# Attention as 64x64 matmul tiles in groups of four, with a two-bank sum for attn·v, two-step lag, and the first two expert blocks in step

## The chip, the cores and the metric

The kernel runs on one core of one Trainium2 chip. The metric is the device time of one execution in microseconds (us). Engines: TensorE (PE; its weight loads are shown apart as PEld), VectorE (DVE), ScalarE (ACT), GpSimd (POOL) and SyncE (SP, which here issues all DMAs). Each of PE, ACT, DVE and POOL works through its own list of instructions in the order in which the kernel writes them, and waits on semaphores for the others.

## The reference

Attention with a sigmoid in place of a softmax, over 8 batches, 12 heads, 448 positions and a head size of 64, and behind it a two-layer feed-forward with a gated ReLU6. All arrays are float32; the two weight matrices come to the kernel as float64 and are converted there.

```python
scores = scale * np.matmul(q, k.transpose(0, 1, 3, 2)) - np.log(S)   # S = 448
attn = 1.0 / (1.0 + np.exp(-scores))
x = np.matmul(attn, v)                       # -> 3584 tokens x 768
h = x @ w_in                                 # 768 -> 2048
g = h * np.clip(h + 3.0, 0.0, 6.0) / 6.0
out = g @ w_out                              # 2048 -> 768
```

## The kernel before, in words

**Stages.** The 3584 tokens are cut into 7 blocks of 512 for the feed-forward, while a batch has 448 tokens. So the program runs: attention of batches 0, 1 and 2; the first layer (`moe_in`, L236 ff.) of blocks 0 and 1; then, for each of batches 3 to 6, its attention and `moe_in` of one block (2 to 5); attention of batch 7; `moe_in` of block 6; and last the second layer (`moe_out`, L378 ff.) of all blocks. Results of the first layer (`g`) go to DRAM and come back for the second.

**Attention.** Two heads share the 128 partitions as a pair `p`: the one's 64 head dimensions in the upper half, the other's in the lower (`halves`). Two pairs make 7 steps `n`: a pair has 448 = 3 x 128 + 64 keys, so three whole chunks each, and one shared step that takes the last 64 keys of both pairs. A batch has 21 steps, and the whole kernel 168.

- `scores(n)` (L153) writes k·q for 128 keys of two heads into a PSUM tile `sc` of two banks. For a whole chunk these are two matmuls with 64 rows (the head size) and 128 columns (the keys), at L163, one per head; they use the upper and the lower half of the array's rows side by side. The shared step uses four matmuls of 64 rows and 64 columns, L161. Then ACT writes the sigmoid of all 2 x 448 columns as `a` to SBUF (L165).
- `av(n)` (L183) multiplies by v and sums over the keys into PSUM `pv` (one bank per pair, `pv0`/`pv1` by parity). For a whole chunk: two matmuls with 128 rows (keys) and 64 columns, L196. In the shared step: four of 64x64, L194.
- The profile shows each float32 matmul as two matmul and two weight-load records. So a whole step has 4 records in `sc` and 4 in `pv`, a shared step 8 and 8.
- When a pair's sum is complete, ACT copies it out rounded to the matmul's type (`xh`, L211), and DVE writes the rest (`xl`, L212). For batch 2 the part that belongs to block 2 waits in `pend` (L208), since block 2's buffers are still those of block 0; `flush` (L175) converts it later.

**Order.** `attention` (L271) goes in groups of `GS` = 3 steps: three `scores`, then the three `av` of the group before, so that there are three `sc` buffers (6 banks) and two `pv` banks. `moe_in` uses the same `sc` buffers for its accumulator `ph`: 18 matmuls of 128x128 by 512 for each of 16 chunks `fc`, then a ReLU on ACT (L250), DVE's product `g` (L251) and the DMA of `g`.

**First-layer weights.** The weights are converted in 32 halves (`load_wi`, L217): DMA of float64 words to `wis` (L230); then ACT (L50), five DVE operations (L51 to L57) and a POOL addition (L60), in `join_f64`; then an ACT cast (L65) and a POOL subtraction (L66) into `wi`, in `split_f32`. `ways` (L257) says when each half does its three parts; `feed` issues them between the steps. 20 halves (`NWA`) belong to the attention of batches 0 to 2, the other 12 to `moe_in(0)`, in units of `KU` = 14 matmuls.

Of the kernel before, what the change touches and what calls it, by code (L numbers as in the profile page):

```python
# [9 lines left out]
F32 = mybir.dt.float32  # L10
# [4 lines left out]
ALU = mybir.AluOpType  # L15

B, H, S, D = 8, 12, 448, 64
DM, DF = 768, 2048
P = 128
NC = S // P  # L20
NP = H // 2
NCC = DM // P
NFC = DF // P
# [5 lines left out]
NB = 3  # L29
PEND = 3 * S - 2 * T  # L30
LC = 2 * NC + 1
LB = NP // 2 * LC
GS = 3
KU = 14
NWA = 20
NWU = 1.4
GSL = 56
NWE = 12
NEA = 5
# [1 line left out]
F64_TOP = float.fromhex("0x1.dfep-96")  # L41

halves = (slice(0, D), slice(D, P))


def join_f64(nc, st, a, b):
# [41 lines left out]
def pieces(b):  # L88

    at, out = b * S, []  # L90
    while at < (b + 1) * S:
        n = min((at // T + 1) * T, (b + 1) * S) - at
        out.append((at // T, at % T, at - b * S, n))
        at += n
    return out
# [3 lines left out]
def tile_kernel(ctx: ExitStack, tc: tile.TileContext, qk, vP, wi, wo, outT):  # L99
    nc = tc.nc  # L100
# [10 lines left out]
    ph2 = ExitStack()  # L111
# [7 lines left out]
        win[g] = wins[g].enter_context(tc.tile_pool(name=f"win{g}", bufs=1, side="right"))  # L119
    xpl = ph2.enter_context(tc.tile_pool(name="xpl", bufs=1))  # L120
    att = ph2.enter_context(tc.tile_pool(name="att", bufs=1))
    ps_s = ph2.enter_context(tc.tile_pool(name="ps_s", bufs=GS, space=bass.MemoryType.PSUM))
    ps_a = ph2.enter_context(tc.tile_pool(name="ps_a", bufs=1, space=bass.MemoryType.PSUM))

    xpr.tile([P, 104], F32, name="pad")
# [7 lines left out]
    ops, at, pv, xb, pend = {}, {}, {}, {}, {}  # L133

    def load(p):
        b, hp = divmod(p, NP)
        t = att.tile([P, 2, S], F32, tag="qk", name=f"qk_{p}", bufs=4)
        v = att.tile([P, 2 * NC + 1, D], F32, tag="v", name=f"v_{p}", bufs=4)
        nc.sync.dma_start(out=t, in_=qk[b, hp])
        if p % 2 == 0:  # L140
            nc.sync.dma_start(out=v, in_=vP[b, hp])
        else:
            nc.sync.dma_start(out=v[:, : 2 * NC], in_=vP[b, hp, :, : 2 * NC])
            for j in range(2):
                nc.sync.dma_start(out=v[halves[1 - j], 2 * NC], in_=vP[b, hp, halves[j], 2 * NC])
        ops[p] = t[:, 0], t[:, 1], v

    def step(n):

        m, r = divmod(n, LC)  # L150
        return ((2 * m, 2 * m + 1), None) if r == NC else ((2 * m + (r > NC),), r % (NC + 1))

    def scores(n):  # L153
        ps, c = step(n)
        sc = ps_s.tile([P, 2, 512], F32, tag="sc", name=f"sc_{n}")
        for u, p in enumerate(ps):
            q, k, _ = ops[p]
            for j in range(2):
                if c is None:
                    out = sc[halves[j if u == 0 else 1 - j], u, :S]  # L160
                    nc.tensor.matmul(out, k[halves[j], NC * P :], q[halves[j]], start=True, stop=True)  # L161
                else:
                    nc.tensor.matmul(sc[:, j, :S], k[halves[j], c * P : (c + 1) * P], q[halves[j]], start=True, stop=True)  # L163
        a = att.tile([P, 2, S], F32, tag="a", name=f"a_{n}", bufs=2 * GS)
        nc.scalar.activation(a, sc[:, :, :S], AF.Sigmoid, bias=bias_s, scale=scale)  # L165
        at[n] = a

    def block(t, cc):
        if (t, cc) not in xb:
            pool = xpl if t % 2 else xpr  # L170
            x = pool.tile([P, 2, T], F32R, tag=f"x{t % 2}{cc}", name=f"x_{t}_{cc}")
            xb[t, cc] = x[:, 0], x[:, 1]
        return xb[t, cc]

    def flush(b, cc):  # L175

        t, c0, _, n = pieces(b)[1]
        xh, xl = (x[:, c0 : c0 + n] for x in block(t, cc))
        x = pend[b][:, cc, :n]
        nc.vector.tensor_copy(xh, x)  # L180
        nc.vector.tensor_tensor(out=xl, in0=x, in1=xh.bitcast(F32), op=ALU.subtract)

    def av(n):  # L183
        ps, c = step(n)
        a = at.pop(n)
        for u, p in enumerate(ps):
            v = ops[p][2]
            if p not in pv:
                pv[p] = ps_a.tile([P, 512], F32, tag=f"pv{p % 2}", name=f"pv_{p}")
            for j in range(2):  # L190
                out = pv[p][halves[j], :S]
                if c is None:
                    rows = halves[j if u == 0 else 1 - j]
                    nc.tensor.matmul(out, v[rows, 2 * NC], a[rows, u], start=(u == 1), stop=(u == 0))  # L194
                else:
                    nc.tensor.matmul(  # L196
                        out, v[:, j * NC + c], a[:, j],
                        start=(p % 2 == 0 and c == 0), stop=(p % 2 == 1 and c == NC - 1),
                    )
        p = ps[0]  # L200
        if c is None or (p % 2 and c == NC - 1):
            b, hp = divmod(p, NP)
            pt = pv[p]
            for u, (t, c0, q0, w) in enumerate(pieces(b)):
                if u and b == NB - 1:
                    if b not in pend:
                        pend[b] = xpl.tile([P, NCC, PEND], F32, tag="pend", name=f"pend_{b}")
                    nc.vector.tensor_copy(pend[b][:, hp, :w], pt[:, q0 : q0 + w])  # L208
                    continue
                xh, xl = (x[:, c0 : c0 + w] for x in block(t, hp))  # L210
                nc.scalar.copy(xh, pt[:, q0 : q0 + w])  # L211
                nc.vector.tensor_tensor(out=xl, in0=pt[:, q0 : q0 + w], in1=xh.bitcast(F32), op=ALU.subtract)  # L212

    wih, wil = {}, {}
    evac = []
# [17 lines left out]
        yield  # L233
        split_f32(nc, hi, lo, ab[:, :w])

    def moe_in(t):  # L236
        for fc in range(NFC):
            if t < NT - 1:
                ph = ps_s.tile([P, 2, T], F32, tag="sc", name=f"ph_{t}_{fc}")[:, 0]
            else:  # L240
                ph = ps_m.tile([P, T], F32, tag="ph", name=f"ph_{t}_{fc}")
            n = 0
            for cc in range(NCC):
                xh, xl = xb[t, cc]
                for w, x in ((wih[fc], xh), (wih[fc], xl), (wil[fc], xh)):
                    nc.tensor.matmul(ph, w[:, cc], x, start=(n == 0), stop=(n == 3 * NCC - 1))  # L246
                    n += 1
                    yield
            g = xpr.tile([P, T], F32, tag="g", name=f"g_{t}_{fc}", bufs=2)
            i1 = nc.scalar.activation(g, ph, AF.Relu, bias=bias_3, scale=1.0)  # L250
            i2 = nc.vector.scalar_tensor_tensor(out=g, in0=g, scalar=6.0, in1=ph, op0=ALU.min, op1=ALU.mult)  # L251
            evac.append((i1.ins, i2.ins))
            nc.sync.dma_start(out=gd[t][fc // GF][:, fc % GF], in_=g)


    NG0 = NB * LB // GS
    ways = []  # L257
    for n in range(2 * NFC):
        i = n * NG0 // NWA
        k = NG0 + 1 + int((n - NWA) * NWU)  # L260
        ways.append((i, i + 2, i + 3) if n < NWA else (k - 3, k, k + 1))
    way = {}

    def feed(part, i):
        for n, parts in enumerate(ways):
            if parts[part] == i:
                if part == 0:
                    way[n] = load_wi(n)
                next(way[n], None)

    def attention(first, last, w_in=False):  # L271

        for s in range(first, last, GS):
            i = (s - first) // GS
            if w_in:
                feed(0, i)
                if s == 0:
                    load(1)
                feed(1, i)
            for n in range(s, s + GS):  # L280
                scores(n)
            if w_in:
                feed(2, i)
            for n in range(s - GS, s):
                if n >= first:
                    av(n)
            for n in range(s, s + GS):
                m, r = divmod(n, LC)
                if r in (0, NC) and (p := 2 * m + 2 + (r == NC)) < B * NP:
                    load(p)  # L290
        for n in range(last - GS, last):
            av(n)

    engines = {mybir.EngineType.PE, mybir.EngineType.Activation, mybir.EngineType.DVE, mybir.EngineType.Pool}
    with tc.manual_schedule(engines=engines):
        load(0)
        attention(0, NB * LB, True)
        for n, _ in enumerate(moe_in(0)):
            i, r = divmod(n, KU)
            if r == 0:  # L300
                for part in range(3):
                    feed(part, NG0 + i)
        for n, _ in enumerate(moe_in(1)):
            if n % (3 * NCC) == 0 and n // (3 * NCC) < NCC:
                flush(NB - 1, n // (3 * NCC))
        for b in range(NB, B):
            attention(b * LB, (b + 1) * LB)
            if b < B - 1:
                for _ in moe_in(b - 1):
                    pass  # L310
# [45 lines left out]
    for n, _ in enumerate(moe_in(NT - 1)):  # L356
        if n % NWE == 0:
            next(early, None)
        g, r = divmod(n, fcm * GF)
# [72 lines left out]
```

## Time and profile before

| | us |
|---|---|
| median of 3 runs | 1212.27 (1211.23 to 1212.77) |
| the profiled execution's own time | 1211.91 |
| its span, first to last instruction | 1210.1 |
| TensorE busy in it | 1200.8 (99%) |
| attention of batches 0 to 2 | 4.27 to 112.37 |
| first layer of blocks 0 and 1 | 112.37 to 243.17 |
| attention of batch 3 | 243.17 to 278.59 |
| last attention (batch 7) starts | 646.87 |
| first layer of block 6 | 683.58 to 749.16 |
| second layer | 749.16 to 1206.41 |

How to read the rows: a group's row names the line, the engine, the operation, the tiles (written <- read), the shape and the count; behind the bar stand the busy time in us and the mean of one in ns, then the idle time of the engine ahead of these instructions and what ended it. Matmuls overlap, so the mean of one matmul is longer than the distance between two. In the chain of work that ended last, each piece has its start, its length and its line; pieces follow each other without a gap. A row of windows has start:end, length, then busy time and count for PE, PEld, DVE, ACT and POOL, the granted clock, the DMA share and GB/s.

### The profile page before, as it was taken

The numbers are of one execution on the slowest core, as the hardware profiler recorded it, in microseconds if no ns is written. First come the engines' busy times: TensorE is split into PE (matmuls) and PEld (weight loads), VectorE is DVE, ScalarE is ACT, GpSimd is POOL, SyncE is SP. The second block draws the span as 40 slices with busy tenths as digits, with TensorE's granted clock in tenths as the row PEclk, the third lists the DMA queues.
The fourth block names the chain that finished last, engine by engine and source line by source line (L and its number), as shares of the span: only waits on it lengthen the run. The fifth ranks groups of instructions, "written<-read, shape, count | busy, mean of one in ns | idle before, by whom it ended". The sixth has DMA issues, their size and how long they took to land.

```text
span 1210.1 us, 13738 instructions
## 1 busy us (share of the span) xinstructions
PE 1200.8 (99%) x5568; PEld 852.4 (70%) x5568; DVE 366.3 (30%) x606; ACT 372.1 (31%) x500; POOL 64.6 (5%) x70
## 2 busy tenths in 40 slices
PE   8999999999999999999999999999999999999998
PEld 3334888837855863883785588888888888888887
DVE  2556742111111111111111389871120303030300
ACT  6886321162144135116214445340110202020200
POOL 1333520000000000000000000000000000000000
PEclk9999999999999999999999999999999999999999
DMA  7666521132133114113212278532040404040000
GB/s 240 193 193 182 158 96 61 69 114 77 61 96 94 70 68 122 61 66 114 80 61 80 79 233 296 211 118 108 29 163 27 157 27 165 27 166 18 27 27 27
DMA packets 52000, 128.84 MB, mean 106 GB/s; under 512 B 9184, under 2 KB 15328, under 8 KB 48352
## 3 DMA queue, kind: packets, MB, share of 16 engines
q1 hardware_dynamic: 51936, 127.95, 31.5%
q8 instruction: 44, 0.72, 0.2%
q14 instruction: 20, 0.16, 0.0%
HBM read 87.56 MB, written 40.37 MB: 106 GB/s over the span
## 4 chain that ended last, share of the span: by engine, by line
PE 99%; DMA 0%; DVE 0%; ACT 0%; issue 0%
PE ph L246 38%; PE po L385 38%; PE sc L163 10%; PE pv L196 10%; PE pv L194 2%; PE sc L161 2%; DMA qk<-qk 0%; DVE o L392 0%; DVE x L212 0%; ACT x L211 0%
## 5 line engine op out<-in xcount | busy, mean ns | idle before, releaser
L246 PE MATMUL ph<-x,wi 128*128 128x512 f32 x2016 | 458.8, 389 | 1.3 <-DVE x L212 1.3
L246 PEld LDWEIGHTS ph<-x,wi 128*128 128x128 f32 x2016 | 377.9, 188 | 83.9 <-issue 3.5
L385 PE MATMUL po<-gl,woh 128*128 128x512 f32 x672 | 261.5, 389 | 0.0
L385 PE MATMUL po<-gh,wol 128*128 128x512 f32 x672 | 261.4, 389 | 0.0
L385 PE MATMUL po<-gh,woh 128*128 128x512 f32 x672 | 261.4, 389 | 0.0
L165 ACT ACTIVATE a<-sc,bias_s 128x896 f32<-128x896 f32 x168 | 157.1, 1007 | 52.4 <-PE sc L163 52.1
L250 ACT ACTIVATE g<-ph,bias 128x512 f32<-128x512 f32 x112 | 77.1, 689 | 294.9 <-PE ph L246 287.9
L251 DVE SCALAR_TENSOR_TENSOR g<-g,ph 128x512 f32<-128x512 f32 x112 | 77.0, 688 | 287.1 <-ACT g L250 287.1
L385 PEld LDWEIGHTS po<-gl,woh 128*128 128x128 f32 x672 | 126.1, 188 | 26.7 <-DVE gl L346 0.4
L345 ACT CAST gh<-gr 128x2048 fp32r<-128x2048 f32 x28 | 53.6, 1915 | 296.5 <-PE po L385 294.8
L385 PEld LDWEIGHTS po<-gh,wol 128*128 128x128 f32 x672 | 126.1, 188 | 26.2
L385 PEld LDWEIGHTS po<-gh,woh 128*128 128x128 f32 x672 | 126.1, 188 | 26.1
L163 PE MATMUL sc<-qk 64*128 64x448 f32 x576 | 127.9, 568 | 4.3 <-DMA qk<-qk 4.3
L196 PE MATMUL pv<-a,v 128*64 128x448 f32 x576 | 122.4, 550 | 0.0
L392 DVE TENSOR_SCALAR o<-po 128x512 f32<-128x512 f32 x42 | 29.0, 690 | 294.9 <-PE po L385 294.9
L163 PEld LDWEIGHTS sc<-qk 64*128 64x128 f32 x576 | 50.6, 189 | 77.7 <-issue 37.3
L196 PEld LDWEIGHTS pv<-a,v 128*64 128x64 f32 x576 | 35.6, 136 | 80.4 <-issue 77.3
L212 DVE TENSOR_TENSOR x<-pv,x 128x448 fp32r<-128x448 f32 (+6 forms) x78 | 32.7, 420 | 195.0 <-ACT x L211 195.0
L346 DVE TENSOR_TENSOR gl<-gr,gh 128x2048 fp32r<-128x2048 f32 x28 | 64.1, 2290 | 29.2 <-ACT gh L345 29.2
L211 ACT CAST x<-pv 128x448 fp32r<-128x448 f32 (+6 forms) x78 | 28.8, 369 | 37.3 <-DVE x L212 14.4
L60 POOL TENSOR_TENSOR wis<-wis 128x384 f32<-128x384 f32 x32 | 32.3, 1010 | 95.6 <-DVE wis L57 95.6
L66 POOL TENSOR_TENSOR wi<-wis,wi 128x384 fp32r<-128x384 f32 x32 | 32.5, 1024 | 7.9 <-ACT wi L65 7.7
(31 smaller groups left out, 307.3 us busy)
## 6 DMA issues: line engine op xcount, KB each, us to landing
gd<-g SPq DMA_DIRECT2D x112, 256.0 KB, 2.4
gr<-gd SPq DMA_DIRECT2D x28, 1024.0 KB, 5.3
qk<-qk SPq DMA_DIRECT2D x48, 448.0 KB, 3.4
wis<-wi SPq DMA_DIRECT2D x32, 384.0 KB, 3.3
ws<-wo SPq DMA_DIRECT2D x24, 512.0 KB, 4.8
outT<-o SPq DMA_DIRECT2D x42, 256.0 KB, 2.0
v<-vP SPq DMA_DIRECT2D x24, 224.0 KB, 2.5
v<-vP SPq DMA_DIRECT2D x24, 192.0 KB, 2.8
```

The lines of the kernel that those rows point to most:

```text
L60: nc.gpsimd.tensor_tensor(out=a, in0=a, in1=b, op=ALU.add)
L66: nc.gpsimd.tensor_tensor(out=lo, in0=a, in1=hi.bitcast(F32), op=ALU.subtract)
L163: nc.tensor.matmul(sc[:, j, :S], k[halves[j], c * P : (c + 1) * P], q[halves[j]], start=True, stop=True)
L165: nc.scalar.activation(a, sc[:, :, :S], AF.Sigmoid, bias=bias_s, scale=scale)
L196: nc.tensor.matmul(out, v[:, j * NC + c], a[:, j], start=(p % 2 == 0 and c == 0), stop=(p % 2 == 1 and c == NC - 1),)
L212: nc.vector.tensor_tensor(out=xl, in0=pt[:, q0 : q0 + w], in1=xh.bitcast(F32), op=ALU.subtract)
L246: nc.tensor.matmul(ph, w[:, cc], x, start=(n == 0), stop=(n == 3 * NCC - 1))
L250: i1 = nc.scalar.activation(g, ph, AF.Relu, bias=bias_3, scale=1.0)
L251: i2 = nc.vector.scalar_tensor_tensor(out=g, in0=g, scalar=6.0, in1=ph, op0=ALU.min, op1=ALU.mult)
L345: nc.scalar.copy(gh, gr)
L346: nc.vector.tensor_tensor(out=gl, in0=gr, in1=gh.bitcast(F32), op=ALU.subtract)
L385: nc.tensor.matmul(po[t, ec], w[:, fc], x[:, u], start=(fc == 0 and n == 0), stop=(fc == NFC - 1 and n == 2))
```

## The change

1. `scores` and `av` use 64x64 tiles only, in the order `TILES` = (rows 0, columns 0), (1, 1), (0, 1), (1, 0). In `scores` the chunk's 128 keys are two column halves, and each head (row half) has its own bank. In `av` the 128 keys are two row halves; each writes a bank of its own, so that a pair has two banks (`pv0_p`, `pv1_p`) that hold two partial sums. Four `pv` banks and two `sc` buffers (4 banks) fill the PSUM.
2. When a pair is complete, ACT copies the one partial sum to SBUF (`y`), DVE adds the other from PSUM (`x`), then DVE casts (`xh`) and subtracts (`xl`). For the pending part the addition goes to `pend`.
3. `attention` goes step by step: `scores(s)`, then `av(s - 2)` (`LAG` = 2), in place of groups of three.
4. `moe_in(0, 1)` runs both blocks together: chunk `fc` of block 0, chunk `fc` of block 1, next chunk. All six `flush` come after it; before, they stood within `moe_in(1)`.
5. The weight schedule is counted in steps: 14 halves in the attention of batches 0 to 2, 18 in `moe_in(0, 1)` at one per 21 matmuls.

```diff
-GS = 3
+LAG = 2
 KU = 14
-NWA = 20
-NWU = 1.4
+NWA = 14
+NWU = 1.5
...
+TILES = ((0, 0), (1, 1), (0, 1), (1, 0))
...
-    ps_s = ph2.enter_context(tc.tile_pool(name="ps_s", bufs=GS, space=bass.MemoryType.PSUM))
+    ps_s = ph2.enter_context(tc.tile_pool(name="ps_s", bufs=2, space=bass.MemoryType.PSUM))
...
     def scores(n):
...
-        for u, p in enumerate(ps):
+        for r, j in TILES:
+            p = ps[-1 if c is None and r != j else 0]
             q, k, _ = ops[p]
...
+            at_k = slice(NC * P, S) if c is None else slice(c * P + j * D, c * P + (j + 1) * D)
+            out = sc[halves[j], int(r != j) if c is None else r, :S]
+            nc.tensor.matmul(out, k[halves[r], at_k], q[halves[r]], start=True, stop=True)
+        a = att.tile([P, 2, S], F32, tag="a", name=f"a_{n}", bufs=LAG + 2)
...
     def av(n):
...
+                pv[p] = [ps_a.tile([P, 512], F32, tag=f"pv{p % 2}{r}", name=f"pv{r}_{p}") for r in range(2)]
+        for r, j in TILES:
+            p = ps[-1 if c is None and r != j else 0]
+            v = ops[p][2][halves[r], 2 * NC if c is None else j * NC + c]
...
+            nc.tensor.matmul(
+                pv[p][r][halves[j], :S], v, a[halves[r], int(r != j) if c is None else j], start=first, stop=last
+            )
...
-                xh, xl = (x[:, c0 : c0 + w] for x in block(t, hp))
-                nc.scalar.copy(xh, pt[:, q0 : q0 + w])
-                nc.vector.tensor_tensor(out=xl, in0=pt[:, q0 : q0 + w], in1=xh.bitcast(F32), op=ALU.subtract)
+                y = att.tile([P, w], F32, tag="y", name=f"y_{p}_{u}", bufs=2)
+                nc.scalar.copy(y, p0[:, q0 : q0 + w])
+                nc.vector.tensor_tensor(out=x, in0=p1[:, q0 : q0 + w], in1=y, op=ALU.add)
+                if not held:
+                    xh, xl = (z[:, c0 : c0 + w] for z in block(t, hp))
+                    nc.vector.tensor_copy(xh, x)
+                    nc.vector.tensor_tensor(out=xl, in0=x, in1=xh.bitcast(F32), op=ALU.subtract)
...
-    def moe_in(t):
-        for fc in range(NFC):
+    def moe_in(*blocks):
+        for fc, t in itertools.product(range(NFC), blocks):
...
-        ways.append((i, i + 2, i + 3) if n < NWA else (k - 3, k, k + 1))
+        ways.append((i, i + 5, i + 8) if n < NWA else (k - 3, k, k + 1))
...
+        for s in range(first, last + LAG):
             if w_in:
+                feed(0, s)
                 if s == 0:
                     load(1)
+                feed(1, s)
+            if s < last:
+                scores(s)
             if w_in:
+                feed(2, s)
+            if s - LAG >= first:
+                av(s - LAG)
...
+        for n, _ in enumerate(moe_in(0, 1)):
...
+        for cc in range(NCC):
+            flush(NB - 1, cc)
```

On PE, in batch 0, this is the row of matmuls around steps 9 to 11 before (`sc_9` are the scores of step 9, `pv_2` the sum of pair 2, `qk_2` its q and k, `a_7` the sigmoid of step 7; a last number counts tiles):

```order
L163 MATMUL sc_9_239<-qk_2_153 128x448 x2
L161 MATMUL sc_10_244<-qk_2_153 64x448 x2
L161 MATMUL sc_10_244<-qk_3_183 64x448 x2
L163 MATMUL sc_11_251<-qk_3_183 128x448 x2
L196 MATMUL pv_1_216<-a_6_202,v_1_133 64x448 x2
L196 MATMUL pv_2_263<-a_7_207,v_2_154 64x448 x2
L196 MATMUL pv_2_263<-a_8_212,v_2_154 64x448 x2
```

And the same place in the changed kernel (`pv0_2` and `pv1_2` are pair 2's two banks):

```order
L162 MATMUL sc_9_282<-qk_2_145 64x448 x4
L194 MATMUL pv0_2_289<-a_7_242,v_2_146 64x448
L194 MATMUL pv1_2_290<-a_7_242,v_2_146 64x448
L194 MATMUL pv0_2_289<-a_7_242,v_2_146 64x448
L194 MATMUL pv1_2_290<-a_7_242,v_2_146 64x448
L162 MATMUL sc_10_295<-qk_2_145 64x448 x2
L162 MATMUL sc_10_295<-qk_3_180 64x448 x2
L194 MATMUL pv0_2_289<-a_8_257,v_2_146 64x448
L194 MATMUL pv1_2_290<-a_8_257,v_2_146 64x448
L194 MATMUL pv0_2_289<-a_8_257,v_2_146 64x448
L194 MATMUL pv1_2_290<-a_8_257,v_2_146 64x448
L162 MATMUL sc_11_312<-qk_3_180 64x448 x4
```

Scores and products alternate step by step, each as a group of four matmuls, where before three steps of the one kind stood ahead of three of the other.

On ACT, this is the order before at the end of batch 2's attention and the start of the first layer (`a_62` is the last sigmoid; `wis_19` on the left of the arrow is the first ACT operation of weight half 19, and `wi_9` read from `wis_18` the cast of half 18; `x_1_5` read from `pv_17` is an eviction; `g_0_0` the first ReLU):

```order
L165 ACTIVATE a_62_986<-sc_62_983,bias_s_117 128x896
L65 CAST wi_8_786<-wis_17_830 128x384
L211 CAST x_1_4_700<-pv_16_955 128x128
L211 CAST x_1_5_738<-pv_17_996 128x128
L50 ACTIVATE wis_19_917<-wis_19_917 128x384
L65 CAST wi_9_874<-wis_18_875 128x384
L50 ACTIVATE wis_20_920<-wis_20_920 128x384
L65 CAST wi_9_874<-wis_19_917 128x384
L250 ACTIVATE g_0_0_1051<-ph_0_0_1011,bias_3_119 128x512
```

The same place in the changed kernel:

```order
L164 ACTIVATE a_62_1261<-sc_62_1256,bias_s_117 128x896
L66 CAST wi_6_1099<-wis_12_1100 128x384
L51 ACTIVATE wis_13_1179<-wis_13_1179 128x384
L51 ACTIVATE wis_14_1230<-wis_14_1230 128x384
L210 COPY y_17_0_1295<-pv0_17_1239 128x128
L210 COPY y_17_1_1300<-pv0_17_1239 128x320
L51 ACTIVATE wis_15_1254<-wis_15_1254 128x384
L66 CAST wi_7_1229<-wis_14_1230 128x384
L66 CAST wi_6_1099<-wis_13_1179 128x384
L66 CAST wi_7_1229<-wis_15_1254 128x384
L253 ACTIVATE g_0_0_1337<-ph_0_0_1303,bias_3_119 128x512
```

Between the last sigmoid and the first ReLU there are now three conversions begun (13, 14, 15) and four casts (12, 14, 13, 15), where before there were two begun (19, 20) and three casts (17, 18, 19). DVE and POOL have their parts of these halves in the same order: DVE those of 13 and 14, then the eviction of pair 17, then that of 15.

More of the change, by code (lines that the diff above doesn't have):

```diff
@@ L155, in scores @@
         sc = ps_s.tile([P, 2, 512], F32, tag="sc", name=f"sc_{n}")
-        for u, p in enumerate(ps):
+        for r, j in TILES:
+            p = ps[-1 if c is None and r != j else 0]
             q, k, _ = ops[p]
[L158 to L164, printed above, removed]
+            at_k = slice(NC * P, S) if c is None else slice(c * P + j * D, c * P + (j + 1) * D)
+            out = sc[halves[j], int(r != j) if c is None else r, :S]
+            nc.tensor.matmul(out, k[halves[r], at_k], q[halves[r]], start=True, stop=True)
+        a = att.tile([P, 2, S], F32, tag="a", name=f"a_{n}", bufs=LAG + 2)
         nc.scalar.activation(a, sc[:, :, :S], AF.Sigmoid, bias=bias_s, scale=scale)
@@ L185, in av @@
         a = at.pop(n)
-        for u, p in enumerate(ps):
-            v = ops[p][2]
+        for p in ps:
             if p not in pv:
[L189 to L199, printed above, removed]
+                pv[p] = [ps_a.tile([P, 512], F32, tag=f"pv{p % 2}{r}", name=f"pv{r}_{p}") for r in range(2)]
+        for r, j in TILES:
+            p = ps[-1 if c is None and r != j else 0]
+            v = ops[p][2][halves[r], 2 * NC if c is None else j * NC + c]
+            whole_first, half_here = p % 2 == 0, (r == j) == (p % 2 == 0)
+            first = p % 2 == 1 if c is None else c == 0 and (whole_first or not half_here)
+            last = p % 2 == 0 if c is None else c == NC - 1 and not (whole_first and half_here)
+            nc.tensor.matmul(
+                pv[p][r][halves[j], :S], v, a[halves[r], int(r != j) if c is None else j], start=first, stop=last
+            )
         p = ps[0]
@@ L202, in av @@
             b, hp = divmod(p, NP)
-            pt = pv[p]
+            p0, p1 = pv[p]
             for u, (t, c0, q0, w) in enumerate(pieces(b)):
-                if u and b == NB - 1:
+                held = u and b == NB - 1
+                if held:
                     if b not in pend:
                         pend[b] = xpl.tile([P, NCC, PEND], F32, tag="pend", name=f"pend_{b}")
-                    nc.vector.tensor_copy(pend[b][:, hp, :w], pt[:, q0 : q0 + w])
-                    continue
-                xh, xl = (x[:, c0 : c0 + w] for x in block(t, hp))
-                nc.scalar.copy(xh, pt[:, q0 : q0 + w])
-                nc.vector.tensor_tensor(out=xl, in0=pt[:, q0 : q0 + w], in1=xh.bitcast(F32), op=ALU.subtract)
+                    x = pend[b][:, hp, :w]
+                else:
+                    x = att.tile([P, w], F32, tag="x", name=f"x_{p}_{u}", bufs=2)
+                y = att.tile([P, w], F32, tag="y", name=f"y_{p}_{u}", bufs=2)
[5 more added lines that the diff above has]
+                    nc.vector.tensor_tensor(out=xl, in0=x, in1=xh.bitcast(F32), op=ALU.subtract)
     wih, wil = {}, {}
@@ L253, in moe_in @@
             nc.sync.dma_start(out=gd[t][fc // GF][:, fc % GF], in_=g)
-    NG0 = NB * LB // GS
+    NS0 = NB * LB
     ways = []
     for n in range(2 * NFC):
-        i = n * NG0 // NWA
-        k = NG0 + 1 + int((n - NWA) * NWU)
-        ways.append((i, i + 2, i + 3) if n < NWA else (k - 3, k, k + 1))
+        i = n * NS0 // NWA
+        k = NS0 + 1 + int((n - NWA) * NWU)
+        ways.append((i, i + 5, i + 8) if n < NWA else (k - 3, k, k + 1))
     way = {}
@@ L271, in attention @@
     def attention(first, last, w_in=False):
-        for s in range(first, last, GS):
-            i = (s - first) // GS
+        for s in range(first, last + LAG):
             if w_in:
-                feed(0, i)
+                feed(0, s)
                 if s == 0:
                     load(1)
-                feed(1, i)
-            for n in range(s, s + GS):
-                scores(n)
+                feed(1, s)
+            if s < last:
+                scores(s)
             if w_in:
[L283 to L292, printed above, removed]
+                feed(2, s)
+            if s - LAG >= first:
+                av(s - LAG)
+            m, r = divmod(s, LC)
+            if s < last and r in (0, NC) and (p := 2 * m + 2 + (r == NC)) < B * NP:
+                load(p)
     engines = {mybir.EngineType.PE, mybir.EngineType.Activation, mybir.EngineType.DVE, mybir.EngineType.Pool}
@@ L296, in tile_kernel @@
         load(0)
-        attention(0, NB * LB, True)
-        for n, _ in enumerate(moe_in(0)):
+        attention(0, NS0, True)
+        for n, _ in enumerate(moe_in(0, 1)):
             i, r = divmod(n, KU)
@@ L301, in tile_kernel @@
                 for part in range(3):
[L302 to L305, printed above, removed]
+                    feed(part, NS0 + LAG + i)
+        for cc in range(NCC):
+            flush(NB - 1, cc)
         for b in range(NB, B):
```

## The prediction

> **What bounds the kernel now.** I read the page's sums first, then the stages by windows, then the chain inside an attention stage. Page: span, busy shares, granted clock, chain that ended last.
>
> ```profile
> span 1210.1 us, 13738 instructions
> PE 1200.8 (99%) x5568; PEld 852.4 (70%) x5568; DVE 366.3 (30%) x606; ACT 372.1 (31%) x500; POOL 64.6 (5%) x70
> ...
> PEclk9999999999999999999999999999999999999999
> ...
> PE 99%; DMA 0%; DVE 0%; ACT 0%; issue 0%
> PE ph L246 38%; PE po L385 38%; PE sc L163 10%; PE pv L196 10%; PE pv L194 2%; PE sc L161 2%; DMA qk<-qk 0%; DVE o L392 0%; DVE x L212 0%; ACT x L211 0%
> ```
>
> TensorE is never without work and its clock is full, so only fewer or shorter TensorE rounds can help. Three quarters of the chain (ph, po) is left alone by the change; sc and pv, 24%, are what it rewrites. The windows give the stages that matter: batches 0 to 2, blocks 0 and 1, and batch 3, which stands for the five single batches.
>
> ```profile
> 4.27:112.37 108.10, 108.10 (x577) 36.80 (x577) 54.03 (x123) 82.99 (x123) 36.86 (x37) 1.00 0.69 209
> 112.37:243.17 130.80, 130.80 (x579) 108.03 (x578) 60.06 (x110) 33.55 (x59) 27.41 (x27) 1.00 0.28 97
> 243.17:278.59 35.42, 35.42 (x194) 11.90 (x193) 4.60 (x11) 23.54 (x32) 0.00 (x0) 1.00 0.39 118
> ```
>
> The chain shows what a busy TensorE hides. Columns: start, length, what; a step is x4 in tall (64x128) or wide (128x64) tiles and x8 in 64x64 tiles.
>
> ```profile
> 4.27 4.52 PE sc L163 x12
> ...
> 253.18 0.91 PE pv L194 x8
> 254.09 1.65 PE pv L196 x8
> 255.74 0.95 PE sc L163 x4
> 256.70 0.91 PE sc L161 x8
> 257.61 0.95 PE sc L163 x4
> 258.56 2.41 PE pv L196 x12
> 260.97 2.46 PE sc L163 x12
> ```
>
> One sc step alone takes 0.95 us, three in a row 2.46: each further step costs (2.46 - 0.95) / 2 = 0.755. For pv, 2.41 - 1.65 = 0.76. What is left is paid whenever the tile shape changes: 0.95 - 0.755 = 0.20 for sc, 1.65 - 2 x 0.76 = 0.13 for pv, 0.91 - 0.755 = 0.155 for the 64x64 steps. A batch has 21 steps of each kind in 8 sc groups, 8 pv groups and 6 shared ones: 42 x 0.755 + 8 x 0.20 + 8 x 0.13 + 6 x 0.155 = 35.3, and the window says 35.42. So about 3.6 us of each batch is changing shape.
>
> **The change, part by part.**
>
> *One tile shape.* All 336 attention groups become what the 64x64 steps are now: four matmuls on four tiles. The streaming (0.755) is the same; the changes of shape go, but for one on entry and the one on leaving, which was there before. That the next group's weights load behind the running one is read from the 64x64 step itself:
>
> ```profile
> 346.55 0.21 PEld L161 LDWEIGHTS sc<-qk 64*64 64x64 f32 x8 [0.65 <-ACT a L165]
> ```
>
> All eight weight loads, those of the second round too, are through 0.21 us after the start of a step of 0.91: they run beside matmuls on the same rows. Batch: 42 x 0.755 + 0.155 = 31.87. No row shows two 64x64 steps in succession, so a group's cost is bounded by 0.755 and 0.91; I take 0.755, since tall and wide steps in succession reach it with loads waiting on the same semaphores.
>
> *Two score buffers instead of three.* At a batch's entry the second sc step now needs the buffer of the last ph. Timeline there:
>
> ```profile
> 344.13 0.69 ACT L250 ACTIVATE g<-ph,bias 128x512 f32<-128x512 f32 x1 [3.39 <-PE ph L246]
> ...
> 344.85 0.69 DVE L251 SCALAR_TENSOR_TENSOR g<-g,ph 128x512 f32<-128x512 f32 x1 [3.39 <-ACT g L250]
> ...
> 345.15 3.70 ACT L165 ACTIVATE a<-sc,bias_s 128x896 f32<-128x896 f32 x4 [0.34 <-PE sc L163]
> ...
> 345.59 0.30 PEld L163 LDWEIGHTS sc<-qk 64*128 64x128 f32 x4 [0.52 <-DVE g L251]
> ```
>
> The buffer is free at 345.59, today just when the third step is due; the second is due at about 344.85. That is a new wait of 0.75 us per batch (bounds 0 and 1.5). Afterwards a score buffer has 3 x 0.755 = 2.27 us between its scores and its next use, and the sigmoid needs 1.0 plus about 0.1 for its release: 1.1 to spare. Batch: 31.87 + 0.75 = 32.62, 2.80 less; five batches 14.0.
>
> *Batches 0 to 2.* 126 groups: 126 x 0.755 + 0.155 = 95.3. The start costs 4.52 - 2.46 = 2.06 more than a warm group, and still does. ScalarE now has less room; its rows and those of the weight conversion (mean ns behind the comma):
>
> ```profile
> L165 ACT ACTIVATE a<-sc,bias_s 128x896 f32<-128x896 f32 x168 | 157.1, 1007 | 52.4 <-PE sc L163 52.1 <-ACT a L165 0.2
> L250 ACT ACTIVATE g<-ph,bias 128x512 f32<-128x512 f32 x112 | 77.1, 689 | 294.9 <-PE ph L246 287.9 <-DMA gd<-g 7.0
> L251 DVE SCALAR_TENSOR_TENSOR g<-g,ph 128x512 f32<-128x512 f32 x112 | 77.0, 688 | 287.1 <-ACT g L250 287.1
> L212 DVE TENSOR_TENSOR x<-pv,x 128x448 fp32r<-128x448 f32 (+6 forms) x78 | 32.7, 420 | 195.0 <-ACT x L211 195.0
> L60 POOL TENSOR_TENSOR wis<-wis 128x384 f32<-128x384 f32 x32 | 32.3, 1010 | 95.6 <-DVE wis L57 95.6
> L211 ACT CAST x<-pv 128x448 fp32r<-128x448 f32 (+6 forms) x78 | 28.8, 369 | 37.3 <-DVE x L212 14.4 <-PE pv L196 12.1 <-PE pv L194 10.6
> L53 DVE SCALAR_TENSOR_TENSOR wis<-wis 128x384 int32<-128x384 int32 x32 | 19.3, 602 | 1.1
> L57 DVE SCALAR_TENSOR_TENSOR wis<-wis 128x384 f32<-128x384 uint32 x32 | 17.9, 558 | 1.1
> L50 ACT ACTIVATE wis<-wis 128x384 f32<-128x384 f32 x32 | 17.9, 558 | 0.0
> L65 ACT CAST wi<-wis 128x384 fp32r<-128x384 f32 x32 | 16.4, 514 | 25.1 <-POOL wis L60 25.1
> L51 DVE TENSOR_SCALAR wis<-wis 128x384 f32<-128x384 f32 x32 | 15.4, 480 | 17.7 <-ACT wis L50 17.3 <-issue 0.4
> L52 DVE TENSOR_SCALAR wis<-wis 128x384 int32<-128x384 int32 x32 | 14.3, 447 | 1.1
> L56 DVE TENSOR_SCALAR wis<-wis 128x384 int32<-128x384 int32 x32 | 11.5, 360 | 1.1
> ...
> L180 DVE CAST x<-pend 128x320 fp32r<-128x320 f32 x6 | 1.9, 321 | 0.0
> ```
>
> Per seven steps (14 x 0.755 = 10.6 us): seven sigmoids 7.05, two evictions of at most two copies of 0.37, so 1.5, and 14/63 x 7 = 1.56 halves of weights at 0.558 + 0.514, so 1.7: 10.2 of 10.6, and less in fact, since four sigmoids in a row take 3.70. It fits, but piles of cast, two copies and conversion (0.51 + 0.74 + 0.56 = 1.8, less the 0.5 that a step leaves) run 1.3 late against 1.1 to spare. I take 0.5 us for all of them (bounds 0 and 5). Sum: 95.3 + 2.06 + 0.5 = 97.9, 10.2 less than 108.10.
>
> *The sum by ACT and DVE.* Per piece of an eviction ACT copies as before; DVE gains an addition (0.42) and a cast (0.32) ahead of its subtraction. The pv bank of a row half is needed again seven groups later, 7 x 0.755 = 5.3 us, and is free after the addition, so this costs nothing on the path. If a conversion (0.48 + 0.45 + 0.60 + 0.36 + 0.56 = 2.45) stands ahead on DVE, it is still about 4.5. At the end of a batch the x of the last pair comes some 0.8 later, but it is read by the 16th of 18 matmuls, 15 x 0.228 = 3.4 us after the first (0.228: 458.8 us over 2016). At the last batch the next stage waits for the pv bank alone, as today; that wait stays.
>
> *Blocks 0 and 1 chunk by chunk.* The same 576 matmuls. The flush of pending x, 6 x 0.8 = 4.9 us of DVE, moves behind them, ahead of batch 3's first eviction, due after 11 groups: nothing. Weights are due every 36 matmuls instead of 18, and loaded one half per 21: no wait. SP issues the same transfers, loads of q, k, v one step earlier or later.
>
> *The junction at batch 2's end costs something.* By the order shown above, ACT has the casts of halves 14, 13 and 15 ahead of the first ReLU, and the cast of 15 needs POOL's addition behind DVE's conversions of 13, 14, the last eviction, and 15. Counted from the first ph, with half 13 starting on DVE then: 3 x 2.45 + eviction (0.42 + 0.32 + 0.42 + 0.42 = 1.6) + POOL 1.0 + cast 0.5 + ReLU 0.7 + g 0.7 = 11.9. With two buffers the third ph wants its buffer after 36 x 0.228 = 8.2: a wait of 3.7. POOL slows DVE beside it:
>
> ```profile
> 115.73 1.06 POOL L60 TENSOR_TENSOR wis<-wis 128x384 f32<-128x384 f32 x1 [5.45 <-DVE wis L57]
> ...
> 115.96 1.05 DVE L52 TENSOR_SCALAR wis<-wis 128x384 int32<-128x384 int32 x1
> ```
>
> 1.05 against a mean of 0.45, 0.6 lost; two such meetings, in part within the means, add 0.8. I take 4.5 (bounds 0 and 8). [...]
>
> **The sum.** 10.2 + 14.0 - 4.5 = 19.7. The profiled span was 1210.1 in an execution of 1211.91, the median of the runs 1212.27. So 1211.91 - 19.7 = 1192.2, by the median 1192.6; I say 1192.5. A measurement of this kernel can tell about 0.2%, 2.4 us, from no change.
>
> **The rivals.**
>
> *The junction is free* (10%): ACT and DVE reach it earlier than I count, or the chain overlaps better. For it: today the two conversions there cost the first ph no wait. Against: three stand there now, with a buffer less. 1192.5 - 4.5 = 1188.
>
> *ScalarE and VectorE hold batches 0 to 2* (17%): piles do not drain, and a late sigmoid holds both sc and pv, since each is fed two steps ahead instead of three. Half of the gain there and 2 us more at the junction: 1192.5 + 5 + 2 = 1199.5. For it: 10.2 of 10.6 by means. Against: 82.99 busy in 108.10 now, with 20 halves where 14 will be. [...]
>
> *Slower: groups of four do not run into each other* (4%). Then each costs 0.91, as the lone ones do: 126 x 0.91 + 2.6 = 117.2, 9.1 more; a batch 42 x 0.91 + 0.75 = 39.0, 3.55 more, five times; with 4.5 at the junction 31 us more: 1243. It decides from about 0.81 per group, where the new waits (0.75 x 5, 4.5, 2.6) eat the gain. For it: no row shows such a succession. Against: the eight loads in 0.21.
> [...]
>
> *It does not run four at a time* (1%): two at a time doubles the groups, 336 x 0.755 = 254 us more. The 64x64 steps of today exclude it nearly.
>
> **The numbers.** The forecast has 65%, with its own range 1188 to 1197. Rivals of the same sign have 27%, those above 1212 6%, and 2% is for no change. The ends are 1183 (no wait at all) and 1205 (all bounds at their worst); 8 in 10 is 1185 to 1200. Faster 0.92, same 0.02, slower 0.06.
>
> **What would show it.** Chain: sc and pv in alternating pieces of 0.75, 31.5 to 32 us per batch beside one wait of 0.75 for DVE g at the second sc; batches 0 to 2 in 97 to 98.5; one wait of 3 to 6 us at the third ph, for DVE g behind ACT's cast for half 15. It is wrong if groups are 0.8 or longer, if sc waits for ACT all through batches 0 to 2, or if ph waits at more than its first chunks.

## The result and the profile after

The changed kernel takes 1193.32 us (median of four runs, 1191.62 to 1193.68), the kernel before 1212.32 (four, 1211.23 to 1212.77): ratio 0.9842, interval 0.9829 to 0.9854. The profiled execution of the changed kernel took 1193.55, so 18.4 us less than the 1211.91 of the profile before; the forecast was 19.7.

The page of the changed kernel: span, busy shares, granted clock, the chain by engine, and the costliest TensorE groups of `moe_in` and of attention.

```profile
span 1191.8 us, 16240 instructions
...
PE 1175.6 (99%) x6720; PEld 857.7 (72%) x6720; DVE 426.8 (36%) x762; ACT 378.6 (32%) x506; POOL 64.3 (5%) x70
...
PEclk9998999999999999999999999999999999999999
...
PE 97%; DVE 1%; ACT 1%; issue 0%; DMA 0%; POOL 0%; DVEq 0%; ACTq 0%
...
L249 PE MATMUL ph<-x,wi 128*128 128x512 f32 x2016 | 461.3, 391 | 5.5 <-DVE g L254 4.2
...
L162 PE MATMUL sc<-qk 64*64 64x448 f32 x1344 | 157.5, 545 | 6.9 <-DMA qk<-qk 4.0
L194 PE MATMUL pv<-a,v 64*64 64x448 f32 x1344 | 154.4, 538 | 0.0
```

TensorE still carries the time, but the chain has left it for 3% of the span, and one digit of the clock row is an 8, where before all were 9. The idle times say where: pv (L194) never waits; sc (L162) waits 6.9, of which 4.0 is the first load of the program; ph (L249) waits 5.5, of which 4.2 is one wait for DVE's `g`. VectorE's 60 us of new work (366.3 before, 426.8 now) stand beside an idle time of 0.0 for pv.

The stages by windows (start:end, length, busy and count of PE, PEld, DVE, ACT, POOL, clock, DMA share, GB/s): batches 0 to 2, the first layer of blocks 0 and 1, and the attention of batch 4.

```profile
3.96:101.72 97.76, 97.76 (x1008) 36.69 (x1008) 64.72 (x140) 81.21 (x119) 25.64 (x26) 1.00 0.66 207
101.72:239.22 137.50, 133.27 (x581) 109.59 (x578) 69.55 (x130) 38.80 (x70) 38.28 (x39) 0.98 0.33 110
...
337.40:369.93 32.53, 31.94 (x337) 12.62 (x337) 10.83 (x31) 24.05 (x32) 0.00 (x0) 1.00 0.41 122
```

Against before:

| term | forecast | measured |
|---|---|---|
| batches 0 to 2 | -10.2 | 97.76 - 108.10 = -10.3 |
| first qk lands earlier | none | 3.96 - 4.27 = -0.3 |
| five batches | -14.0 | 5 x (32.53 - 35.42) = -14.4 |
| first layer of blocks 0 and 1 | +4.5 | 137.50 - 130.80 = +6.7 |
| sum | -19.7 | -18.3 |

The chain of the changed kernel (start, length, what; a group of four tiles is x8), at the program's start and at the entry into a batch:

```profile
3.96 4.76 PE sc L162 x24
8.71 1.38 PE pv L194 x8
10.09 0.75 PE sc L162 x8
...
338.13 0.70 DVE g L254
...
338.88 1.73 PE sc L162 x16
340.61 0.75 PE pv L194 x8
...
345.12 0.75 PE pv L194 x8
```

Groups of four tiles run into each other: from 340.61 to 345.87 (the end of the last row) are seven, 0.7514 each. Where a stage is slower than that, it is at its edges. At the start four groups take 6.13 (3.96 to 10.09) instead of 3.01. At the entry the chain runs over DVE's `g`. The timeline of the changed kernel shows that entry and, above it, the junction where the first layer begins (start, length, engine, line, operation; in brackets the idle time before and what ended it):

```profile
99.69 0.23 DVE L214 CAST x<-x 128x128 fp32r<-128x128 f32 x1
...
101.72 8.46 PE L249 MATMUL ph<-x,wi 128*128 128x512 f32 x36
...
102.42 0.36 DVE L53 TENSOR_SCALAR wis<-wis 128x384 int32<-128x384 int32 x1
...
104.44 1.06 POOL L61 TENSOR_TENSOR wis<-wis 128x384 f32<-128x384 f32 x1 [2.27 <-DVE wis L58]
104.67 1.05 DVE L53 TENSOR_SCALAR wis<-wis 128x384 int32<-128x384 int32 x1
...
107.54 0.93 DVE L214 CAST x<-x 128x128 fp32r<-128x128 f32 x1
...
111.52 0.99 POOL L61 TENSOR_TENSOR wis<-wis 128x384 f32<-128x384 f32 x1 [3.13 <-DVE wis L58]
...
112.54 0.51 ACT L66 CAST wi<-wis 128x384 fp32r<-128x384 f32 x1 [3.19 <-POOL wis L61]
112.96 0.68 ACT L253 ACTIVATE g<-ph,bias 128x512 f32<-128x512 f32 x1
...
113.67 0.69 DVE L254 SCALAR_TENSOR_TENSOR g<-g,ph 128x512 f32<-128x512 f32 x1 [2.23 <-ACT g L253]
...
114.42 10.86 PE L249 MATMUL ph<-x,wi 128*128 128x512 f32 x37 [4.23 <-DVE g L254]
...
337.31 0.98 PE L162 MATMUL sc<-qk 64*64 64x448 f32 x8
...
338.88 1.73 PE L162 MATMUL sc<-qk 64*64 64x448 f32 x16 [0.59 <-DVE g L254]
```

The junction reads from bottom to top: the third ph starts at 114.42, when `g` (113.67) has left its buffer; `g` waited for the ReLU (112.96), the ReLU stood behind the cast of the last half (112.54), and that behind POOL's addition (111.52). The two ph before were done at 110.18. At the entry the second sc group starts 1.57 after the first instead of 0.75, so 0.8 are lost; the view counts 0.59 of it as idle, since it shows the lone group as 0.98 long.

The wait at the junction has a sequel. Windows of the changed kernel around it; the clock stands third from the end:

```profile
112.00:115.00 3.00, 0.58 (x1) 0.50 (x2) 1.29 (x3) 2.12 (x4) 3.00 (x4) 0.54 0.21 26
115.00:119.00 4.00, 4.00 (x11) 3.12 (x10) 3.86 (x7) 1.07 (x2) 1.51 (x2) 0.50 0.90 322
119.00:122.00 3.00, 3.00 (x15) 2.47 (x14) 1.75 (x4) 0.94 (x2) 1.29 (x2) 0.99 0.29 113
```

TensorE pauses from 110.18 on. Some 2 us later the clock falls to half, and it stays there to about 119.0, while TensorE works again from 114.42: 4.6 us at half speed, 2.3 lost. The pause is 4.23 by the view and 0.16 that the view hides (the 0.391 of a mean matmul less the 0.228 between two). 4.23 + 0.16 + 2.3 is the 6.7 of the table.

### The profile page after: what moved, and what is told of

The parts are those of the page before. It is cut to its first block, busy times and chain, and to the rows that moved or that the text cites. A ratio compares the mean times of both kernels' runs of the same rounds, so it can differ in the third digit from the quotient of the medians.

```text
span 1191.8 us, 16240 instructions
## 1 busy us (share of the span) xinstructions
PE 1175.6 (99%) x6720; PEld 857.7 (72%) x6720; DVE 426.8 (36%) x762; ACT 378.6 (32%) x506; POOL 64.3 (5%) x70
## 4 chain that ended last, share of the span: by engine, by line
PE 97%; DVE 1%; ACT 1%; issue 0%; DMA 0%; POOL 0%; DVEq 0%; ACTq 0%
PE po L382 38%; PE ph L249 38%; PE sc L162 11%; PE pv L194 10%; DVE g L254 0%; ACT g L253 0%; DMA qk<-qk 0%; DVE wis L53 0%; DVE wis L54 0%; DVE wis L52 0%; ACT y L210 0%; DVE wis L57 0%; POOL wis L61 0%; DVE x L214 0%; DVE x L211 0%
## 5 line engine op out<-in xcount | busy, mean ns | idle before, releaser
L249 PE MATMUL ph<-x,wi 128*128 128x512 f32 x2016 | 461.3, 391 | 5.5 <-DVE g L254 4.2
L249 PEld LDWEIGHTS ph<-x,wi 128*128 128x128 f32 x2016 | 379.5, 189 | 89.1 <-DVE g L254 4.7
L164 ACT ACTIVATE a<-sc,bias_s 128x896 f32<-128x896 f32 x168 | 168.5, 1007 | 54.5 <-PE sc L162 53.2
L162 PE MATMUL sc<-qk 64*64 64x448 f32 x1344 | 157.5, 545 | 6.9 <-DMA qk<-qk 4.0
L194 PE MATMUL pv<-a,v 64*64 64x448 f32 x1344 | 154.4, 538 | 0.0
L162 PEld LDWEIGHTS sc<-qk 64*64 64x64 f32 x1344 | 49.6, 134 | 85.4 <-issue 56.2
L194 PEld LDWEIGHTS pv<-a,v 64*64 64x64 f32 x1344 | 50.3, 134 | 76.7 <-issue 71.9
L211 DVE TENSOR_TENSOR x<-pv,y 128x448 f32<-128x448 f32 (+6 forms) x78 | 32.4, 415 | 114.3 <-ACT y L210 93.9
L215 DVE TENSOR_TENSOR x<-x,x 128x448 fp32r<-128x448 f32 (+6 forms) x78 | 32.8, 420 | 2.7
```

The source lines that it names most:

```text
L162: nc.tensor.matmul(out, k[halves[r], at_k], q[halves[r]], start=True, stop=True)
L194: nc.tensor.matmul(pv[p][r][halves[j], :S], v, a[halves[r], int(r != j) if c is None else j], start=first, stop=last)
L211: nc.vector.tensor_tensor(out=x, in0=p1[:, q0 : q0 + w], in1=y, op=ALU.add)
```

## Experiments

The theory after this result: the gain is the shape changes that are gone; what keeps it from being larger is one pause at the junction and the clock behind it, and an entry wait per batch. Rivals: the gain came from the new order rather than from the shape; ScalarE holds batches 0 to 2; the slow clock has a cause of its own. Measured times are medians, and each ratio stands against runs of the kernel before on the same chip (median 1212.62 beside runs 1 to 4, 1212.39 beside 5 to 7). Sums use the profiled executions, one of each kernel, while the executions of one kernel spread by 0.9 to 5 us; where a sum meets the difference of two whole executions to a tenth, chance has a part in it, and the stage times carry the argument.

**1. Only the scores of whole chunks back to tall tiles** (64 rows by 128 columns), all else as changed:

```diff
+        if c is not None:
+            q, k, _ = ops[ps[0]]
+            for j in range(2):
+                nc.tensor.matmul(sc[:, j, :S], k[halves[j], c * P : (c + 1) * P], q[halves[j]], start=True, stop=True)
-        for r, j in TILES:
+        for r, j in TILES if c is None else ():
```

> The changed kernel, but the scores of whole chunks go back to two matmuls of 64 rows and 128 columns; products, order, banks and eviction stay. Theory (the gain is the tile-shape changes that no longer happen): every whole step has its shape changed twice again, 0.95 for the scores and 0.91 for the product as the lone groups of before have, 1.86 instead of 1.50, 144 times: 51 us more, about 1244. Rival (the gain comes from alternating step by step and from lag 2, with any shapes): 1193 to 1200.

Measured: 1240.79 us, ratio 1.0234 (1.0215 to 1.0252): slower than the kernel before. Its chain within a batch (here L160 is the tall form, L198 the product):

```profile
263.00 0.95 PE sc L160 x4
263.95 0.91 PE pv L198 x8
...
274.19 0.75 PE sc L166 x8
```

Every piece now pays for a change of shape: 0.95 and 0.91, where 0.75 stands as soon as two groups of the same shape follow each other (the last row, a shared step behind a product). A batch has sixteen stretches of tall groups (its first three scores stand together, and the three shared steps are square) and sixteen of square ones, not the eighteen that were expected: 8 x 16 x (0.20 + 0.16) = 46. The profiled executions differ by 47.7, with 1.3 of a new wait at the start of the second layer in it. This is shown: the order is the changed kernel's, and with mixed shapes it loses all of the gain and more. The order with step-by-step alternation pays only because there is one shape. What one shape would give in the old order, three steps of a kind at a time, was not run.

**2. The weight halves due later at the junction**: 12 halves in batches 0 to 2, and the first of the other 20 five units into the first layer, so that no conversion stands ahead of the first ReLU:

```diff
-NWA = 14
+NWA = 12
...
-        k = NS0 + 1 + int((n - NWA) * NWU)
+        k = NS0 + 5 + int((n - NWA) * NWU)
```

> The changed kernel with 12 instead of 14 weight halves in batches 0 to 2 and the rest begun 4 units of 14 matmuls later, so that no conversion stands ahead of the first ReLU. Theory (three conversions ahead of the first ReLU hold the third ph, and the pause lowers the clock for some us): wait of 4.2 and 2.3 of slow matmuls go, granted clock 1.000, about 1186.8. Rival (two ph buffers behind the last eviction are too few by themselves): a wait of 2 to 4 us stays at the third ph, 1190 to 1193.

Measured: 1186.91, ratio 0.979 (0.9777 to 0.9804). The chain of this run has the whole first layer in one piece:

```profile
101.65 130.80 PE ph L249 x576
```

130.80 is what this stage took before the change, to the digit. So the conversions ahead of the first ReLU cost 6.7, and nothing else in that stage does.

**3. One unit later only**, to make the pause shorter without removing it:

```diff
-        k = NS0 + 1 + int((n - NWA) * NWU)
+        k = NS0 + 2 + int((n - NWA) * NWU)
```

> The changed kernel with the halves from 14 on begun one unit of 14 matmuls later. The conversion of 14 then follows the last eviction and that of 15 still stands ahead of the first g. Theory for the wait: about 2.5 us at the third ph instead of 4.2. For the clock two theories: it falls only after a long pause, then no slow matmuls here and about 1189.3; or it falls after any pause of us, then about 1191.6 with some 1.4 us of slow matmuls.

Measured: 1188.42, ratio 0.9801 (0.9788 to 0.9815). Its timeline at the third ph, and its window behind that:

```profile
111.60 8.70 PE L249 MATMUL ph<-x,wi 128*128 128x512 f32 x37 [1.92 <-DVE g L254]
```

```profile
111.60:118.00 6.40, 6.40 (x28) 5.30 (x29) 4.67 (x8) 2.69 (x5) 4.49 (x5) 1.00 0.73 196
```

A pause of 1.92, a clock of 1.00 behind it, and 1188.71 - 1186.64 = 2.07 more than without a pause (profiled executions of this run and of run 2): just the pause, with its hidden 0.16. Conversions run beside this pause too, and the clock stays full behind it: in the changed kernel the slow clock came with the longer pause (4.23), not with the work at the junction. That length alone does not decide is what run 6 shows.

**4. ph in the pv banks**, which are idle in the first layer, for blocks 0 to 5: four buffers at the junction instead of two, and the score buffers free at each entry:

```diff
-                ph = ps_s.tile([P, 2, T], F32, tag="sc", name=f"ph_{t}_{fc}")[:, 0]
+                i = fc * len(blocks) + blocks.index(t)
+                ph = ps_a.tile([P, T], F32, tag=f"pv{i // 2 % 2}{i % 2}", name=f"ph_{t}_{fc}")
```

> The changed kernel, but ph of blocks 0 to 5 takes the four pv banks in turn instead of the two score buffers. Theory: the junction has four buffers, so its wait and the slow clock go (6.5 us); at the entry of batches 3 to 7 the second scores no longer wait for g, but then the third scores come due before the first sigmoid is done behind the last ReLU, so the 0.6 us per entry stays with ACT as its releaser: about 1186.8. Rival: the entry wait is the lack of a free buffer alone and goes too, 2.9 us more: about 1183.9.

Measured: 1187.52, ratio 0.9797 (0.9784 to 0.981). What TensorE still waits for in this run (in total, times, longest):

```profile
PE sc L162 <- ACT a L164: 1.9, 5, 0.4
PE po L383 <- DVE gl L344: 1.5, 1, 1.5
```

The junction's wait is gone without touching the schedule of the weights. The entry's did not go, it moved: the third sc group now waits 0.4 for the first sigmoid, since two score buffers cannot hold three groups. A wait of 1.5 at the start of the second layer is new; run 1 has one of 1.3 there with ph in the score buffers, so it is not shown to come from the pv banks. Together: 6.7 + 5 x 0.2 - 1.5 = 6.2 gained, and 1193.55 - 1187.29 = 6.3 is what the profiled executions differ by.

**5. Blocks 0 and 1 one after the other**, with 20 halves in batches 0 to 2 at 1.4 per unit, as before the change; the tiles and the step order as changed:

```diff
-NWA = 14
-NWU = 1.5
+NWA = 20
+NWU = 1.4
...
-        for n, _ in enumerate(moe_in(0, 1)):
+        for n, _ in enumerate(moe_in(0)):
...
+        for _ in moe_in(1):
+            pass
```

> The changed kernel with that one part undone: block 0, then block 1, with 20 weight halves in batches 0 to 2 and 12 in block 0 at one per 19.6 matmuls, as before the change. Theory (running the blocks together buys room for ACT and DVE, no TensorE time): ACT has 10.4 to 10.9 us of work for 10.6 us of matmuls per seven steps, so 0 to 3 us of waits in batches 0 to 2; the third ph waits 4 to 7 us with some us of low clock as in the changed kernel, and block 0 adds 0 to 5 us of waits for g, since a half now comes every 4.4 us with two ph buffers: about 1198 (1194 to 1204). Rival: the order of the blocks is neutral, 1193.

Measured: 1203.37, ratio 0.9931 (0.9914 to 0.9948). Its windows of batches 0 to 2 and behind the wait at the third ph, and its waits:

```profile
4.15:106.82 102.67, 100.18 (x1008) 39.73 (x1008) 85.34 (x166) 85.61 (x129) 35.32 (x35) 1.00 0.63 207
124.07:132.00 7.93, 7.93 (x29) 6.44 (x30) 4.83 (x9) 3.09 (x6) 4.51 (x5) 0.81 0.68 220
```

```profile
PE ph L249 <- DVE g L254: 8.8, 1, 8.8
...
PE sc L162 <- ACT a L164: 1.6, 2, 0.9
```

That is inside the expected 1194 to 1204, but 5 above the 1198 named. With six more halves batches 0 to 2 are longer by 4.9 (102.67 against 97.76; 2.5 of it shows as idle, 102.67 - 100.18, of which 1.6 in two waits for ACT's sigmoid and 0.7 in two for DVE's `x`), where 0 to 3 were expected, and the junction's wait by 4.6 (8.8 against 4.2), where 4 to 7 in all were. The further waits for `g` in block 0 did not come. Of the half clock more now lies inside the longer pause: 7.93 x 0.19 = 1.5 lost behind it instead of 2.3. So with 20 halves ScalarE and VectorE do hold TensorE in that stage, with 14 they do not. By the profiled executions the tiles and the step order with the blocks apart gain 1211.91 - 1202.40 = 9.5 of the 18.4 us, and running the two blocks together, with the schedule of halves that goes with it, adds 8.9; by the medians it is 9.0 and 10.0 of 19.0. The run does not part the order of the blocks from the schedule: the chain at the junction's wait here holds two loads of weight halves (3.22 from 104.98, 3.09 from 116.66), and the changed kernel's chain there holds none.

**6. ACT's copy of each piece done twice** (84 copies more; the second writes the same values), to see how much room ScalarE has:

```diff
                 nc.scalar.copy(y, p0[:, q0 : q0 + w])
+                nc.scalar.copy(y, p0[:, q0 : q0 + w])
```

> The changed kernel with every ACT copy of a partial sum done twice (84 more, 0.37 us each, 31 us of ACT in all), to see what room ACT has. Theory: nothing in batches 3 to 7, where ACT has 0.5 us to spare per step; in batches 0 to 2 some 11.2 us of ACT for 10.6 us of matmuls per seven steps, so 4 to 6 us in all: about 1198. If the eviction were on the path everywhere: up to 31 us, 1224. If ACT had room everywhere: 1193.

Measured: 1200.45, ratio 0.9898 (0.9883 to 0.9913). Windows of this run (batches 0 to 2, batch 4, the wait before block 6 and behind it), two of its waits, and its chain at the end of batch 4:

```profile
4.29:104.09 99.80, 98.83 (x1008) 37.71 (x1009) 64.02 (x140) 90.04 (x147) 25.52 (x26) 1.00 0.64 204
...
340.72:373.76 33.04, 32.19 (x337) 12.54 (x337) 10.83 (x31) 26.68 (x42) 0.00 (x0) 1.00 0.42 127
...
668.00:672.00 4.00, 2.13 (x16) 1.03 (x13) 2.52 (x5) 1.22 (x3) 0.00 (x0) 0.99 0.35 83
672.00:676.00 4.00, 4.00 (x13) 3.09 (x12) 0.93 (x3) 0.66 (x1) 0.00 (x0) 0.58 0.78 314
```

```profile
PE ph L250 <- DVE x L212: 1.9, 1, 1.9
PE pv L194 <- ACT a L164: 1.3, 5, 0.3
```

```profile
370.47 0.37 ACT y L210
...
371.50 0.32 ACT y L211
371.81 0.92 ACT a L164
...
372.78 0.98 PE pv L194 x8
```

By the profiled executions it costs 7.1 (1200.69 - 1193.55), more than the expected 4 to 6, and in other places. 8.8 us more of ScalarE's time (90.04 - 81.21) cost batches 0 to 2 only 2.0 (99.80 - 97.76). Each of the five later batches, where nothing was expected, lost 0.5 (33.04 against 32.53): the chain shows four copies in a row (370.47 to 371.81) ahead of the last sigmoid, and the last product waiting for that. The last wait grew from 1.3 to 1.9, and behind it the clock fell to half for a while, 4 x 0.42 = 1.7. So ScalarE has some room in the stage with the weights, and none at the ends of batches.

**7. Runs 2 and 4 together, and the third scores of batches 3 to 7 in the pv banks** (`pv10` and `pv11`, with a sigmoid for each bank), so that nothing is left to wait for at the entries:

```diff
+        if n >= NB * LB and n % LB == 2:
+            banks = [ps_a.tile([P, 512], F32, tag=f"pv1{r}", name=f"sc{r}_{n}") for r in range(2)]
...
+            for r in range(2):
+                nc.scalar.activation(a[:, r], banks[r][:, :S], AF.Sigmoid, bias=bias_s, scale=scale)
...
+                i = fc * len(blocks) + blocks.index(t)
+                late = i >= NFC * len(blocks) - 4
+                ph = ps_a.tile([P, T], F32, tag=f"pv{(i // 2 + late) % 2}{i % 2}", name=f"ph_{t}_{fc}")
```

> The version with later weight halves (1186.9), and besides ph of blocks 0 to 5 in the four pv banks, with the third scores of batches 3 to 7 in the two pv banks that are still free there. Theory (at an entry TensorE waits for the lack of a third score tile, whoever releases it): 0.6 us per entry go, 2.9 us, about 1184.0. Rival: another release is just behind, and 0.4 us per entry stay, about 1186.

Measured: 1186.77, from 1183.86 to 1188.82 in four runs, ratio 0.9787 (0.9769 to 0.9804). All waits of TensorE for another engine or a load in its profiled execution (the 1183.86), and an entry in its timeline:

```profile
PE sc L166 <- DMA qk<-qk: 4.2, 1, 4.2
...
PE ph L259 <- DVE x L219: 1.3, 1, 1.3
PE po L392 <- DVE gl L353: 1.1, 1, 1.1
```

```profile
329.05 2.48 PE L166 MATMUL sc<-qk 64*64 64x448 f32 x24
```

Three groups run through the entry in 2.48, so the five entry waits are gone. The profiled execution is 2.8 shorter than run 2's, but not all of that is the change: 0.6 lies in batches 0 to 2, which the two kernels run alike (the first layer begins at 101.06 against 101.65), and against the 5 x 0.8 of the entries stand the new 1.1 at the second layer and some 0.7 elsewhere that was not traced. Over its runs it spreads by 5 us, and its median is no better than run 2's 1186.91, nor near the expected 1184. Where the other runs lose it is not settled: the new wait at the second layer, of runs 1, 4 and 7 alike, hangs on loads of `g` and of the second weights, and may vary, but only one execution was profiled. Runs 2, 4 and 7 all beat both kernels; run 2 does it with two constants and the narrowest spread of the three.

## Why the prediction was right, and where its sum was off

*One tile shape* was right in mechanism and size. Groups of four cost 0.7514 in succession, against the 0.755 taken and the bound of 0.91; run 1 puts the shape changes back and loses 48 us. With this the rival of groups that do not run into each other falls. In the 6% above 1212 stands 1% for groups that each show their weight loads as well. No run shows such groups: in the changed kernel a group has two rows of four loads, 0.14 each (97.12 and 97.49 in the group of 97.11), that lie beside matmuls, and groups in a row take a bare 0.7514.

*The entry wait* was right: 0.75 forecast, 0.8 measured, for DVE's `g` at the second sc group; five batches gave 14.4 for 14.0.

*Batches 0 to 2* came out at 97.76 for 97.9, by errors that cancel: the start costs 97.76 - 126 x 0.7514 = 3.1 more than warm groups, not 2.06 (the fourth group, a pv, is slow too); ACT's piles cost nothing, not 0.5; and the groups came 0.6 below the 95.3 taken for them. That it met the forecast to a tenth is luck, the more so as the same start cost 1.9 in run 7. For ACT's piles run 6 shows that there was room: 8.8 us more for ScalarE cost 2.0. The rival that ScalarE and VectorE hold this stage is what happens with 20 halves (run 5), not with 14.

*The junction* is the mis-sized term, 6.7 for 4.5. The mechanism stood in the forecast, in the right place and order: third ph behind `g`, the ReLU, the cast of half 15, POOL. The wait itself came to 4.23 + 0.16 for the 4.5, by two errors that cancel: DVE's two meetings with POOL cost 0.7 each (1.05 for 0.36, 0.93 for 0.23), 1.4 instead of the 0.8 taken, and the rest of the chain was some 0.6 shorter than counted. What the forecast did not have is that TensorE, after such a pause, works on at half clock for a while (0.50 from 115 to 119, 2.3 us lost). Runs 2 and 3 show both: no pause, 130.80; a pause of 1.92, the pause and no more, at a clock of 1.00.

*The additions of DVE, the flush, the order of the blocks* cost TensorE nothing, as forecast: pv waits 0.0, and the last wait, before block 6, is 1.3 as before. That running the blocks together, with its schedule of halves, is worth 8.9 us (run 5) was in the forecast only as 14 halves instead of 20, without a number.

## What to carry to other kernels

When a saturated TensorE alternates between tile shapes, read the price of a change from the chain (a lone group against groups in a row, here 0.95 against 0.755) and count the changes; here a finer tile that is the same everywhere beat a larger one (1193.32 against 1212.32), and only together with all its neighbours (run 1, 1240.79). The pause of TensorE at the junction had two prices, its length (4.4) and the half clock behind it (2.3), while the 1.92 of run 3 had only the first and the 1.9 of run 6 both; look for such a pause where a buffer is taken away and background work stands ahead of the engine that frees it. Moving that work by a few units (run 2) was worth a third of the whole change.

## What the runs showed of the hardware

**The clock after a pause.** Pauses of TensorE and the granted clock behind them: 1.92 (run 3), 1.00; 4.0 (run 1), 4.2 (the changed kernel) and 8.8 (run 5), lower for a while: 0.50 from 115 to 119 in the changed kernel, in the mean 0.90 from 125 to 135 in run 1 and 0.81 from 124.07 to 132 in run 5. In the changed kernel half clock begins 2 us into the pause (1.00 from 111 to 112, 0.62 from 112 to 113) and lasts nearly 7 us; in run 5 it begins about 5 us into the pause, an estimate from its means (0.74 from 117 to 130, 0.81 from 124.07 to 132) that takes the clock as either full or half. But the 1.9 before block 6 in run 6 brought it too, only after TensorE had started again (0.99 to 672, 0.58 behind it). So near 1.9 the length of a pause alone does not decide; what else does, no run shows.

**DVE beside POOL.** The junction's timeline has DVE's operation at L53 at 0.36 when alone (102.42) and at 1.05 beside POOL's addition (104.44 and 104.67), which was expected. Not expected was that DVE's new cast of an evicted piece (L214), 0.23 alone (99.69), takes 0.93 at 107.54 beside the next addition of POOL (1.01 from 107.38): of the steps that this eviction gained on DVE, one was caught by POOL.

**The start.** The first four groups take 3.1 us more than warm ones at a granted clock that the profile gives as full (1.00 from 3.96 to 10.09). In run 7, which begins with the same groups, they take 1.9 more (4.19 to 9.10). No run here shows why, nor what sets the difference.
